# Three edits to the first microseconds of a linear-attention and MLP kernel: a table load put first on ScalarE, one weight load moved to SyncE's queue, and fewer filler products

## The chip, the core and the metric

The kernel runs on one core of one Trainium2 chip. The metric is the device time of one execution in microseconds (us); the time of a kernel is the median of its runs. A profile is one further execution, taken with the hardware profiler, and it has a time of its own. In the profile PE is TensorE (PEld its weight loads), DVE is VectorE, ACT is ScalarE, POOL is GpSimd and SP is SyncE. A name with a q behind it (SPq, ACTq) is the engine's sequencer, which issues DMAs. The granted TensorE clock is 1.000 in the profiled execution.

## What is computed

```python
x = A_x                                     # [1, 2048, 640], bf16
g = _sigmoid((x * gate_w).sum(-1, keepdims=True))
a = _A_ref(x, A_wqkv, A_wo)                 # linear attention, 32 heads of 20
b = _B_ref(x, B_w1, B_w2, B_w3, B_w4)       # layernorm, w1, gelu, shifted columns, w2, layernorm, w3, gelu, w4
return g * a + (1 - g) * b

# in _A_ref:
phi = lambda t: jnp.where(t > 0, t + 1, jnp.exp(t)) + 1e-6
pq, pk = phi(q), phi(k)
kv = jnp.einsum("bhsd,bhse->bhde", pk, v)
...
```

All inputs are bf16. The products with `wqkv`, `w1`, `w2`, `w3` and `w4` fill TensorE's time. The exponential in `phi` is the first function that ScalarE needs, and it needs a table for it; the gelu of the second half needs another.

## The kernel before, in words

**Tiles.** The 2048 rows of `x` are 16 tiles of 128 tokens. `x_tok[:, t, :]` holds tile `t` with tokens on the partitions, and `xT` holds the same data turned, 640 = 5 slices of 128 features by 2048 tokens. `wq` and `wkg` hold the q and k columns of `wqkv`, each in 5 slices of 128 rows. A q tile is 5 products (one for each slice) of 512 columns, summed in one PSUM bank. The remaining 128 columns of `wq` come later as one strided load.

**Who issues the first loads.** The program writes the DMA issues of the first tiles out by hand (lines 714 to 739). `load_x(t)` always issues on SP. `load_wq(k, queue)` and `load_wk(k, queue)` issue on the queue that is named. Each engine's sequencer issues in the order of the program, and each DMA has a semaphore of its own, on which its first reader waits. SP's order is x tile 0, x tile 1, `wq` slice 2, x tile 2, `wkg` slices 0 and 2, x tile 3, `wkg` slice 4, x tile 4. ACT's order is `wq` slices 0, 1, 3 and 4, `wkg` slices 1 and 3, and then the strided rest of `wq`. An x tile and a `wkg` slice are 160 KB each, and a slice of `wq` is 128 KB. From tile 3 on the tiles are turned by DMA transposes (`x_turn`, line 711), also on SP, each of which waits for its tile.

**What TensorE does meanwhile.** `warmup(WARM, ...)` (line 896) multiplies constants into a PSUM bank that nobody reads: with `WARM` = 3456 it is six products of 512 columns and three of 128. `t_x(t)` (line 798) turns tiles 0, 1 and 2 on TensorE (five 128x128 transposes each, against `ident`), and DVE copies the result from PSUM to `xT`. `q_three` (line 949) runs the first three q tiles in an order written out by hand:

```python
order = [(0, 0), (1, None), (0, 1), (1, 0), (1, 1), (0, 2), (1, 2), (0, 3), (1, 3), (2, None), (0, 4), (1, 4),
         (2, 0), (2, 1), (2, 2), (2, 3), (2, 4)]
```

A pair (t, k) is the product of tile `t` with slice `k` of `wq`, and (t, None) is `t_x(t)`. `stream` (line 926) issues them in this order, and TensorE does them in it, so each entry waits for what its own operands need and holds up all behind it. `k_two` (line 958) does the same for the first two k tiles with `wkg`, and `k_tile` and `q_tile` follow, one tile after another.

**The order of the rest.** `_Items.run` (line 336) orders the remaining work by a small cost model (`_Sched.simulate`): the stream A, in which the start lies, keeps its own order, and the other streams are put between by estimated times. `activation` (line 669) tells the model that the first Exp and the first Gelu cost 1290 ns more, for the load of the table. The instruction that loads the table, ACT_TABLE_LOAD, stands in ACT's program directly before the first activation that needs it.

The lines that the change and the prediction touch are 714 to 739, 795, 798, 896 and 949. DMA issues all have line 285 in the profile, since a helper records them (transposes 281); PE's fillers have line 904, its transposes 637, and the products of `stream` 942.

Of the kernel before, what the change touches and what calls it, by code (L numbers as in the profile page):

```python
# [6 lines left out]
F32 = mybir.dt.float32  # L7
ACTF = mybir.ActivationFunctionType
# [408 lines left out]
def _build(nc, A_x, A_wqkv, A_wo, B_w1, B_w2, B_w3, B_w4, gate_w, out, dbg=None, stop=None):  # L417
# [66 lines left out]
    junk = pa.alloc("junk", [128, 1, D], BF16)  # L484
# [78 lines left out]
    def nfree(ap):  # L563
        n = 1
        for d_ in ap.shape[1:]:
            n *= d_
        return n

    def in_psum(ap):
        return ap.tensor.name == ps.name  # L570

    def act(fn, reads, writes, cost=None):
        if cost is None:
            n = nfree(writes[0])
            cost = max(150.0, 100.0 + 0.833 * n + (70.0 if (reads and in_psum(reads[0])) else 0.0))
            cost += 45.0 * max(0, len(reads) - 1)
        return sch.op("act", fn, reads, writes, cost=cost)

    def dve(fn, reads, writes, cost=None):
        if cost is None:  # L580
            n = nfree(writes[0])
            cost = 65.0 + n / 0.96
        return sch.op("dve", fn, reads, writes, cost=cost)
# [85 lines left out]
    def activation(out_ap, in_ap, func, scale=1.0, bias=0.0, accum=None):  # L669
        rd = [in_ap] + [a for a in (scale, bias) if not isinstance(a, (int, float))]  # L670
        wr = [out_ap] + ([accum] if accum is not None else [])
        n = nfree(out_ap)
        cost = max(150.0, 100.0 + 0.833 * n + (70.0 if in_psum(in_ap) else 0.0)) + 45.0 * (len(rd) - 1)
        if accum is not None:
            cost += 91.0
        st_ = ACT_SET.get(func)
        if st_ is not None and st_ != sch.act_func:
            cost += 1290.0
            sch.act_func = st_
        if accum is not None:  # L680
            return act(lambda e: e.activation(out_ap, in_ap, func, bias=bias, scale=scale, accum_out=accum), rd, wr, cost=cost)  # L681
        return act(lambda e: e.activation(out_ap, in_ap, func, bias=bias, scale=scale), rd, wr, cost=cost)  # L682
# [16 lines left out]
    def dma_in(out_ap, in_ap, key, **kw):  # L699
        return sch.dma("sp", out_ap, in_ap, key, **kw)  # L700

    def load_x(t):
        dma_in(x_tok[:, t, :], x2[128 * t:128 * (t + 1), :], "x%d" % t)

    def load_wq(k, queue):
        sch.dma(queue, wq[:, k, 0:512], A_wqkv[128 * k:128 * (k + 1), 0:512], "wq%d" % k)
# [6 lines left out]

    gwr = xn[:, 1, 0:128]
    dve(lambda e: e.memset(gwr, 0.0), [], [gwr])
    load_x(0)
    load_wq(0, "act")
    load_x(1)
    load_wq(1, "act")
    load_wq(2, "sp")  # L720
# [71 lines left out]
        assert tags.get((buf, sl)) == what, ("stale ring slot", buf, sl, what, tags.get((buf, sl)))  # L792

    IT = _Items()
    WARM = 3456
    WARM2 = 128

    def t_x(t):
        for k0, k1 in ((0, 1), (1, KD)) if t < 2 else ((0, KD),):
            b = bank()  # L800
            tr_group(b, [x_tok[:, t, 128 * k:128 * (k + 1)] for k in range(k0, k1)])
            if t == 2:
                mm_group(ps[:, b, 448:448 + KD], [(gwr, ident[:, 0:KD])])
            for j0, j1 in {(1, 1): ((1, 3), (3, KD)), (2, 0): ((0, 1), (1, 3), (3, KD))}.get((t, k0), ((k0, k1),)):
                copy(dve, xT[:, j0:j1, 128 * t:128 * (t + 1)], psb(b, 128 * (j0 - k0), 128 * (j1 - k0)).rearrange("p (k c) -> p k c", k=j1 - j0))
            if t == 2:
                copy(dve, wkg[:, :, D + 1:D + 2], ps[:, b, 448:448 + KD].rearrange("p (k o) -> p k o", o=1))
# [88 lines left out]
    def warmup(cols, cyc):  # L896
        b = bank()
        one = nc.const_aps.tensor(1.0, [128, 512], BF16)
        steps = [512] * (cols // 512) + [128] * (cols % 512 // 128)

        def fn(e):
            ins = None
            for n in steps:
                ins = e.matmul(ps[:, b, 0:n], one[:, 0:128], one[:, 0:n], start=True, stop=True)
            return ins
        pe(fn, [], [ps[:, b, :]], cost=cols * cyc)
# [54 lines left out]
    def addA(name, dur, fn, deps=()):  # L961
        IT.add("A", name, dur, fn, deps)

    addA(("warm",), 0.0, lambda: warmup(WARM, 0.834))
    addA(("tx", 0), 0.28, lambda: t_x(0))
# [485 lines left out]
def bass_gated_mix__linear_attn_block__mixer_s_mlp__prompt_kernel(  # L1451
    nc, A_x, A_wqkv, A_wo, B_x, B_w1, B_w2, B_w3, B_w4, gate_w, out
):
    assert tuple(A_x.shape) == (1, S, D) and tuple(out.shape) == (1, S, D)
    assert tuple(A_wqkv.shape) == (D, 3 * D) and tuple(A_wo.shape) == (D, D)
    assert tuple(B_w1.shape) == (D, D) and tuple(B_w2.shape) == (D, D)
    assert tuple(B_w3.shape) == (D, F) and tuple(B_w4.shape) == (F, D) and tuple(gate_w.shape) == (D,)
    _build(nc, A_x, A_wqkv, A_wo, B_w1, B_w2, B_w3, B_w4, gate_w, out)
# [28 lines left out]
```

## Time and profile before

| what | value |
|---|---|
| runs | 258.79 us median of 3 (258.46 to 259.11) |
| the profiled execution | 259.12 us, of it a span of 257.9 us from the first to the last instruction |
| busy | PE 254.6 us (99% of the span), DVE 144.1, ACT 108.5, POOL 90.6 |
| chain that ended last | PE 96%, DMA 2% |
| first DMA issues | 0.79 us on SP and on ACT |
| fillers | 0.83 us to about 3.7 us |
| ACT_TABLE_LOAD, the first of two | 4.14 us, 1.28 us long |
| first Exp | 8.01 us |

The span is cut into instructions of each engine. Times in the timeline count from the span's start. A DMA issue has a start and a length on the sequencer (0.40 to 0.46 us for these), and apart from it a time to landing, from the start of the issue to the last step of its semaphore. The chain that ended last is followed back from the last instruction; what stands in it sets the end, and other work has slack.

### The profile page before, as it was taken

The page shows a single profiled execution, that of the slowest core. Times are in us where ns is not written, and L with a number is a line of the kernel's source. Part 1 is how long each engine was busy: PE and PEld are TensorE (multiplying, and loading weights), DVE is VectorE, ACT ScalarE, POOL GpSimd, SP SyncE. Part 2 cuts the span into 40 slices and gives each one's busy share as a digit, 9 for nine tenths or more (in the row PEclk, how much of TensorE's full clock was granted, in tenths as well). Part 3 has the DMA queues.
Part 4 walks back from the last instruction along what each step waited for, and adds up shares of the span by engine and source line. Part 5 has one row for each costly group of instructions (what it writes and reads, how often), then busy time and mean ns, then how long its engine had stood idle before and what let it go on. Part 6 is the DMA issues. An engine that isn't in the chain of part 4 may idle for free.

```text
span 257.9 us, 3612 instructions
## 1 busy us (share of the span) xinstructions
PE 254.6 (99%) x1418; PEld 110.6 (43%) x1242; DVE 144.1 (56%) x290; ACT 108.5 (42%) x222; POOL 90.6 (35%) x146
## 2 busy tenths in 40 slices
PE   8999999999999999999999999999999999999997
PEld 4333333344454333334444444444444444444444
DVE  2697888899953995489999400689300043200033
ACT  1486676751356867665854230003520100253000
POOL 5021399967762153758907100423000011300000
DMA  6767698545843699362915520022300112200002
GB/s 209 223 170 197 145 144 223 172 86 127 108 99 78 97 335 382 85 106 51 124 40 127 127 54 20 0 82 73 51 0 0 23 20 102 102 1 3 0 20 102
DMA packets 57825, 26.48 MB, mean 103 GB/s; under 512 B 49188, under 2 KB 56397, under 8 KB 57808
## 3 DMA queue, kind: packets, MB, share of 16 engines
q1 hardware_dynamic: 54976, 21.87, 35.9%
q0 software_dynamic: 1168, 3.28, 4.9%
q10 hardware_dynamic: 1664, 1.11, 1.4%
q8 instruction: 10, 0.16, 0.3%
q14 instruction: 7, 0.06, 0.1%
HBM read 12.04 MB, written 2.62 MB: 57 GB/s over the span
## 4 chain that ended last, share of the span: by engine, by line
PE 96%; DMA 2%; SPq 0%; DVE 0%; issue 0%
PE ps L606 37%; PE ps L1240 30%; PE ps L625 14%; PE ps L831 7%; PE ps L614 4%; DMA x_tok<-in_A_x_dram 2%; PE ps L942 1%; PE ps L1286 1%; PE ps L1147 1%; SPq L285 0%; PE ps L1029 0%; PE ps L1058 0%; PE ps L637 0%; DVE x_tok L665 0%
## 5 line engine op out<-in xcount | busy, mean ns | idle before, releaser
L606 PE MATMUL ps<-xnT,w 128*128 128x512 bf16 x360 | 81.3, 379 | 0.0
L665 DVE SCALAR_TENSOR_TENSOR x_tok<-ps,stg,abx 128x512 bf16<-128x512 f32 (+2 forms) x17 | 12.2, 719 | 81.5 <-PE ps L1240 81.3
L682 ACT ACTIVATE h2T<-ps 128x512 bf16<-128x512 f32 x52 | 30.6, 598 | 59.3 <-PE ps L606 59.3
L606 PEld LDWEIGHTS ps<-xnT,w 128*128 128x128 bf16 x360 | 34.5, 98 | 41.6 <-issue 2.2
L1240 PE MATMUL ps<-w,h2T 128*128 128x512 bf16 (+2 forms) x221 | 45.4, 366 | 0.0
L648 POOL TENSOR_SCALAR xn<-x_tok,st 128x640 bf16<-128x640 bf16 x32 | 35.3, 1110 | 27.8 <-DMA xnT<-xn 27.2
L648 POOL TENSOR_SCALAR abx<-x_tok,stg 128x640 f32<-128x640 bf16 (+1 forms) x16 | 14.8, 930 | 70.0 <-DVE x_tok L665 70.0
L1240 PEld LDWEIGHTS ps<-w,h2T 128*128 128x128 bf16 x221 | 21.1, 98 | 24.1
L682 ACT ACTIVATE Er<-ps 128x512 bf16<-128x512 f32 (+1 forms) x36 | 23.0, 648 | 14.8 <-PE ps L614 10.6
L681 ACT ACTIVATE junk<-x_tok 128x640 bf16<-128x640 bf16 x32 | 23.6, 738 | 3.9 <-DVE x_tok L663 3.7
L682 ACT ACTIVATE hsT<-ps 128x512 bf16<-128x512 f32 (+1 forms) x32 | 19.0, 593 | 12.6 <-PE ps L606 12.1
L625 PE MATMUL ps<-w,hsT 128*128 128x512 bf16 x80 | 23.0, 379 | 0.0
L625 PE MATMUL ps<-wkg,xT 128*128 128x512 bf16 x70 | 20.6, 379 | 0.0
L663 DVE SCALAR_TENSOR_TENSOR x_tok<-ps,x_tok 128x640 bf16<-128x640 f32 x16 | 13.2, 822 | 10.8 <-PE ps L614 10.2
L1240 PE MATMUL ps<-M_sb,pqnT 128*128 128x512 bf16 (+2 forms) x85 | 18.6, 367 | 0.0
L831 PE MATMUL ps<-pk_tok,x_tok 128*128 128x512 bf16 x80 | 17.8, 379 | 0.0
L614 PE MATMUL ps<-wkg,xT 128*128 128x130 bf16 x80 | 17.6, 220 | 0.0
L1176 DVE TENSOR_TENSOR pq_tok<-pq_tok,dnr 128x300 bf16<-128x300 bf16 (+1 forms) x48 | 17.3, 415 | 0.6
L614 PE MATMUL ps<-w,hsT 128*128 128x128 bf16 x80 | 17.5, 219 | 0.0
L606 PE MATMUL ps<-wq,xT 128*128 128x512 bf16 x65 | 16.2, 379 | 0.0
L648 DVE TENSOR_SCALAR Er<-Er 128x512 bf16<-128x512 bf16 (+1 forms) x36 | 12.2, 340 | 6.8 <-ACT Er L682 5.9
L656 DVE TENSOR_TENSOR qprod<-qprod,pk_tok 128x640 f32<-128x640 f32 x13 | 15.1, 1165 | 0.4
(90 smaller groups left out, 252.4 us busy)
## 6 DMA issues: line engine op xcount, KB each, us to landing
w<-in_B_w_dram SPq DMA_DIRECT2D x1, 2160.0 KB, 8.1
w<-in_B_w_dram SPq DMA_DIRECT2D x1, 2080.0 KB, 13.1
out_dram<-x_tok SPq DMA_DIRECT2D x3, 640.0 KB, 3.1
w<-in_B_w_dram POOLq DMA_DIRECT2D x8, 160.0 KB, 3.4
x_tok<-in_A_x_dram SPq DMA_DIRECT2D x6, 160.0 KB, 4.1
x_tok<-in_A_x_dram SPq DMA_DIRECT2D x1, 960.0 KB, 5.5
wv<-in_A_wqkv_dram POOLq DMA_DIRECT2D x1, 800.0 KB, 5.3
x_tok<-in_A_x_dram SPq DMA_DIRECT2D x1, 640.0 KB, 5.0
```

What stands on the lines that cost most here:

```text
L606: ins = e.matmul(out_ap, l, r, start=(i == 0), stop=(i == n - 1))
L614: return e.add_instruction(mybir.InstMatmult(name=nc.get_next_instruction_name(), engine=e.engine, ins=[e.lower_ap(r), ll], outs=[e.lower_ ...
L625: e.matmul(outs[0], l, r, start=st, stop=sp, skip_group_check=True)
L648: return engf(lambda e: e.tensor_scalar(out_ap, in_ap, s1, s2, op0, op1), rd, [out_ap], cost=cost)
L656: return engf(lambda e: e.tensor_tensor(out_ap, a, b_, op), [a, b_], [out_ap], cost=cost)
L663: return dve(lambda e: e.scalar_tensor_tensor(out_ap, in0, scalar, in1, op0, op1, accum_out=accum), rd, [out_ap, accum], cost=cost + 70.0)
L665: return dve(lambda e: e.scalar_tensor_tensor(out_ap, in0, scalar, in1, op0, op1), rd, [out_ap], cost=cost)
L681: return act(lambda e: e.activation(out_ap, in_ap, func, bias=bias, scale=scale, accum_out=accum), rd, wr, cost=cost)
L682: return act(lambda e: e.activation(out_ap, in_ap, func, bias=bias, scale=scale), rd, wr, cost=cost)
L831: ins = e.matmul(o, l, r, start=(t0 + q_ == 0), stop=(t0 + q_ == NT - 1))
L1176: dve(lambda e, o=o, i0=i0, i1=i1: e.tensor_tensor(o, i0, i1, ALU.mult), [i0, dnr[:, 1, sd, :]], [o], cost=cost)
L1240: ins = e.matmul(o, l, r, start=first and i == 0, stop=last and i == len(prs) - 1, skip_group_check=True)
```

## The change

ScalarE's program gets one activation in front: an Exp of one constant column (128x1) into `junk`, which nobody reads. With it the table load moves from behind ACT's seven DMA issues to before them. The load of `wq` slice 0 goes from ACT's queue to SP's, behind x tile 0 and ahead of x tile 1. `WARM` becomes 3200, which is six products of 512 columns and one of 128.

```diff
     gwr = xn[:, 1, 0:128]
     dve(lambda e: e.memset(gwr, 0.0), [], [gwr])
+    activation(junk[:, 0, 0:1], nc.const_aps.tensor(0.0, [128, 1], F32), ACTF.Exp)
     load_x(0)
-    load_wq(0, "act")
+    load_wq(0, "sp")
     load_x(1)
     load_wq(1, "act")
     load_wq(2, "sp")
...
     IT = _Items()
-    WARM = 3456
+    WARM = 3200
     WARM2 = 128
```

SP's order is then x tile 0, `wq` slice 0, x tile 1, `wq` slice 2, x tile 2, `wkg` slices 0 and 2, and so on; ACT's is table load, Exp, `wq` slices 1, 3 and 4, `wkg` slices 1 and 3, the strided rest of `wq`.

## The prediction

> **What bounds the kernel now.** I read the page's chain first, then the chain at the start in order of time.
>
> ```profile
> ## 4 chain that ended last, share of the span: by engine, by line
> PE 96%; DMA 2%; SPq 0%; DVE 0%; issue 0%
> ```
>
> ```profile
> 2.18 5.05 DMA x_tok<-in_A_x_dram
> 7.23 0.05 issue
> 7.28 0.45 PE ps L637 x5
> ```
>
> From 7.28 us on the chain is nearly all PE, and the page has PE busy 99% of the span: whatever moves PE's work at 7.28 moves the end by as much. What PE waits for there is x tile 2, which SP issues at 2.18 and which lands at 7.23. PE itself shows the wait:
>
> ```profile
> 7.28 0.45 PE L637 MATMUL ps<-ident,x_tok 128*128 128x128 bf16 x5 [0.55 <-DMA x_tok<-in_A_x_dram]
> 7.57 0.17 PE L606 MATMUL ps<-ident,xn 128*128 128x5 bf16 x1
> 7.60 1.74 PE L942 MATMUL ps<-wq,xT 128*128 128x512 bf16 x7
> ```
>
> PE was idle for 0.55 us (by modelled ends; the last product before, (1,3), starts at about 6.35, so by starts it could have gone on at 6.57). So everything before 7.28, fillers included, has slack, and the question is when x tile 2, or another operand, lands. Next the two issuing queues, in order of time:
>
> ```profile
> 0.79 0.87 SPq L285 DMA_DIRECT2D x_tok<-in_A_x_dram  x2
> 1.71 0.43 SPq L285 DMA_DIRECT2D wq<-in_A_wqkv_dram  x1
> 2.18 0.43 SPq L285 DMA_DIRECT2D x_tok<-in_A_x_dram  x1
> 2.66 0.91 SPq L285 DMA_DIRECT2D wkg<-in_A_wqkv_dram  x2
> ```
>
> ```profile
> 0.79 1.86 ACTq L285 DMA_DIRECT2D wq<-in_A_wqkv_dram  x4
> 2.69 0.94 ACTq L285 DMA_DIRECT2D wkg<-in_A_wqkv_dram  x2
> 3.65 0.46 ACTq L285 DMA_DIRECT2D wq<-in_A_wqkv_dram  x1
> 4.14 1.28 ACT L682 ACT_TABLE_LOAD   x1 [4.14 <-issue]
> 8.01 1.09 ACT L682 ACTIVATE Er<-ps 128x512 bf16<-128x512 f32 x2 [2.59 <-PE ps L942]
> ```
>
> Each issue takes about 0.46 us, and the table load lies in ACT's idle time: its first Exp waits for PE until 8.01, 2.59 us after the load is over. Last, the DMA view narrowed to one issue at a time (here SP's third, fourth and fifth: the last number is the time to landing), and the stretches of the windows view:
>
> ```profile
> wq<-in_A_wqkv_dram SPq DMA_DIRECT2D x1, 128.0 KB, 3.6
> ...
> x_tok<-in_A_x_dram SPq DMA_DIRECT2D x1, 160.0 KB, 5.1
> ...
> wkg<-in_A_wqkv_dram SPq DMA_DIRECT2D x1, 160.0 KB, 5.5
> ```
>
> ```profile
> 3.20:4.00 0.80, 0.80 (x7) 0.55 (x6) 0.00 (x0) 0.00 (x0) 0.65 (x4) 1.00 1.01 342
> 4.00:4.80 0.80, 0.80 (x9) 0.59 (x8) 0.56 (x2) 0.66 (x1) 0.72 (x5) 1.00 1.00 292
> 4.80:5.60 0.80, 0.80 (x9) 0.42 (x6) 0.79 (x4) 0.62 (x1) 0.00 (x0) 1.00 0.89 253
> ```
>
> The last two columns are the share of the DMA engines and GB/s. With a share of 0.9 to 1.0 the loads are bound by the DMA engines, not by their issue. Issue plus time to landing gives SP's landings: x0 3.7, x1 4.4, wq2 5.3, x2 7.2, wk0 8.1 or 8.2, wk2 8.9, x3 9.5, wk4 10.1 us; and ACT's, read in the same way: wq0 3.8, wq1 4.6, wq3 5.6, wq4 7.5, wk1 8.3, wk3 9.1, the rest of wq 10.9 us. Two queues side by side each land one DMA in about 0.6 to 1.9 us, so a DMA's time is its place in its own queue.
>
> **The change, part by part.**
>
> *wq0 on SP.* SP gets one issue more ahead of x1, wq2 and x2. x2 becomes SP's fifth DMA and takes the place of wk0. The bytes say the same: before, SP's first five are 160+128+160+160+160 = 768 KB, after, 160+128+160+128+160 = 736 KB; ACT's first five are 672 KB before and, one place further on, 384+160+160 = 704 KB after. Both sums are 1440 KB. So x2 lands where wk0 does now, 8.1 instead of 7.23: +0.9 us. A second chain ends at the same moment: wq2 takes x2's place, 7.2, and behind it PE still has (0,2), (1,2), (0,3), (1,3), four products at 0.216 us from start to start, to 8.1. This is why x2 being asked for by issue only 0.47 us later is not the price: the lower bound is 0.47, the upper one the place of wk0 by its rounded row, 2.66+5.5-7.23 = 0.93, and I take 0.9, since the DMA engines' share is near 1. Behind it nothing is late: wk0 then lands at 8.9 and is first read at 9.18+0.9, wk4 at 10.6 (x4's place) and is read at about 11.1+0.9; x3 lands at 10.1, its transpose took 2.5 us to land, and q tile 3 starts at 13.26+0.9.
>
> The Trainium skill, "DMA: Bandwidth & Descriptors", section "Issuing engines are not separate DMA queues", says that transfers from all issuing engines share the same DMA engines, and that the issuing engine decides only over the sequencer's time. By that alone this part would cost one issue, +0.47 us instead of +0.9, and the whole would stay within 0.3%.
>
> *Table load first.* It takes 1.28 us off ACT at 4.14, where ACT was idle, so nothing is won there. It puts 1.28 us and an Exp of one column (nearest row: the 128x2 activation at 12.16, 0.17 us) ahead of ACT's issues. Does ACT's sequencer wait for them? No DMA stands behind an ACT compute instruction in the early trace. The nearest row: a semaphore instruction of ACT's sequencer ends at 13.1 us while the Exp that starts at 12.93 runs to 13.63. The sequencer goes on while the engine works. I therefore take about nothing for the issues: wq1 goes out at 0.8 to 0.9, into wq0's old place. The other end, 1.28 us and more, is the first rival; the table load is another kind of instruction than the Exp, so that end stays likely.
>
> *256 columns of filler fewer.* Two products of 128 columns, which start 0.11 us apart while the clock is still slow: PE is free 0.21 us earlier, at about 3.5. x0 lands at 3.7 as before, so the 0.21 us become a wait for x0; and if x0 came earlier, the gain would end at x2's wait. Cost nothing, cover the wait for x2. The fillers' other effect is the clock: 512 columns start 0.43 us apart up to 3.35, and 0.216 apart from 4.95 on, and weight loads fall from 151 to 98 ns at about 4.3. In the forecast PE also idles from about 4.4 to 5.3 (x1 in wq2's place). If that put the fast clock off, the products before 8.1 would hide it; behind 8.1 each would cost 0.2 us more. I price this at nothing, with up to +0.4 us in the range (two products).
>
> *The planner's costs* move by 1290 ns on ACT and 0.2 us on PE at the start. Stream A keeps its order, and from the middle on all engines are shifted alike; I take nothing, and 0.2 us either way.
>
> Sum: +0.9 us. The profiled execution has 259.12 (span 257.9 and 1.2 around it), so it would have 260.0; it lies 0.33 above the median of the runs. On the median, 258.79+0.9 = 259.7 us. What a measurement of this kernel can tell from no change is about 0.3%, 0.78 us.
>
> **The rivals.**
>
> *First, faster: the table load holds ACT's issues.* Then ACT issues wq1 at 0.79+1.28 = 2.07, and SP has the DMA engines almost alone until about 3.1 us (wq0, issued at 0.79, needed 3.0 us). x0, wq0, x1 land early, and x2 before it is needed. wq1 lands at 2.07+3.0 = 5.1, about when (0,1) ran (4.95); wq3 and wq4 follow after 288 KB each of the two queues' traffic, at some 360 GB/s 0.82 us: 5.9 and 6.7. (0,3) and (1,3) end by 6.5, `t_x(2)` runs without a wait, and (0,4) starts at 6.75 instead of 7.60: -0.85 us, 257.9. PE's own work sets the floor: 6.57 plus the 0.32 us from 7.28 to 7.60, less 0.21 of filler, is 6.7. If wq4 keeps its old gap behind wq3 (1.9 us), (0,4) is at 7.6 or later and the gain is none, so this rival's price runs from -0.95 to 0. For it speaks that the load at 68.30 starts 0.02 us after the Activation before it ended, as if the sequencer waited for the engine (plain Activations of that stretch stand no further apart); against it the semaphore row. It decides from a delay of ACT's issues of about 1 us on.
>
> The Trainium skill, "ScalarE: Activation LUTs", section "What ACT_TABLE_LOAD costs", gives 1.28 us for the load and 1.38 us of drain with it, 2.66 in all; the trace shows 1283 ns and no drain. An estimate by that page would put wq1's issue at 3.45, wq4 at 8.1 and this rival 0.5 us slower than before instead of faster.
>
> *Second, no change: the load disturbed the transfers.* Between 4.0 and 5.6, about where the table load ran (4.14 to 5.42), the rate fell from 342 to 292 and 253 GB/s. DVE's copies ran there as well. If the load was the cause, its move gives back (50+89) GB/s x 0.8 us = 111 KB, at 350 GB/s 0.32 us, and the sum is +0.9-0.3 = +0.6, 259.4 us.
>
> **How the numbers follow.** The forecast has 0.52, and with its bounds (+0.5 to +1.3) 0.42 of that is over 0.78 us and 0.10 within. The first rival has 0.38: 0.28 beyond 0.78 us, 0.10 within. The second has 0.10, 0.05 within, 0.03 slower, 0.02 faster where the relief adds to the first. That makes 0.30 faster, 0.25 within 0.3%, 0.45 slower. The range reaches from the first rival's -0.95 (257.8) to the forecast's +1.3, which is 0.9 and the clock's 0.4 (260.1); the forecast's own range is 259.3 to 260.1.
>
> **What would show it.** Forecast: ACT's first DMA issue starts by 1.0 us, wq2 lands near 7.2, x2 near 8.1, and the first transposes of `t_x(2)` start there instead of at 7.28, the rest shifted alike. First rival: ACT's first issue starts after 2.0 us, x2 lands before 6.5, and PE's wait, if any, is for wq3 or wq4. Second: the first DMA issue is early and the rate between 4.0 and 5.6 stays over 320 GB/s. The prediction is wrong altogether if the chain's first long wait is neither x2 nor a slice of wq, or if PE's time from `t_x(2)` to the end changes by over 0.3 us.

## The result, and the profile after

The changed kernel takes 261.35 us (median of 10 runs, 259.57 to 262.01), the kernel before 258.91 us in the 10 runs beside it. The ratio is 1.0073, with a 95% interval of 1.0051 to 1.0095, which is 1.9 us slower (1.3 to 2.5); by the medians it is 2.4 us, because most runs of the changed kernel are in the upper one of two groups. The forecast was 0.9. The groups are 3 runs at 259.57 to 259.68 us and 7 at 261.05 to 262.01. The runs before have no second group (258.32 to 259.42). The profiled execution, 261.42 us with a span of 260.1, is of the upper group.

The page's chain, and then the chain at the start in order of time (start, length, what):

```profile
PE 94%; DMA 2%; ACT 2%; DVE 1%; issue 1%; SPq 0%
```

```profile
1.71 4.78 DMA x_tok<-in_A_x_dram
6.49 0.05 issue
6.54 0.71 PE ps L637 x5
7.25 2.59 PE ps L943 x7
```

The DMA that ends PE's wait is now the one issued at 1.71, x tile 1. Behind it PE is the chain from 6.54 on: tile 2's transposes, which ended the wait before, come after the products without a wait. PE's own view (start, length, what, and the idle time ahead of it) shows two things:

```profile
4.47 0.58 PE L943 MATMUL ps<-wq,xT 128*128 128x512 bf16 x1 [0.18 <-DMA wq<-in_A_wqkv_dram]
6.54 0.71 PE L637 MATMUL ps<-ident,x_tok 128*128 128x128 bf16 x5 [1.49 <-DMA x_tok<-in_A_x_dram]
7.04 2.79 PE L943 MATMUL ps<-wq,xT 128*128 128x512 bf16 x7
9.68 0.44 PE L637 MATMUL ps<-ident,x_tok 128*128 128x128 bf16 x5
9.95 0.17 PE L606 MATMUL ps<-ident,xn 128*128 128x5 bf16 x1
9.98 1.74 PE L943 MATMUL ps<-wq,xT 128*128 128x512 bf16 x7
```

PE idles 1.49 us for tile 1. Then seven products of 512 columns take 2.79 us behind tile 1 and seven others 1.74 us behind tile 2, and five transposes 0.71 and 0.44 us. Behind tile 1 the products start 0.43 us apart up to 9.18 us, as the fillers of 512 columns do at the start, and behind tile 2 mostly 0.22 us apart. This is what "half speed" and "slow clock" mean here: until about 9.2 us TensorE takes twice the time for the same work. Tile 2's transposes start at 9.68 instead of 7.28, and the first k product at 11.56 instead of 9.18.

ACT's issues did not wait for the table load:

```profile
0.79 1.28 ACT L682 ACT_TABLE_LOAD   x1 [0.79 <-PEq L1473]
0.86 1.35 ACTq L285 DMA_DIRECT2D wq<-in_A_wqkv_dram  x3
```

And in the DMA view, one issue at a time, these are SP's third and fifth, x tiles 1 and 2 (issued at 1.71 and 2.66, so they land at 6.5 and 7.9):

```profile
x_tok<-in_A_x_dram SPq DMA_DIRECT2D x1, 160.0 KB, 4.8
...
x_tok<-in_A_x_dram SPq DMA_DIRECT2D x1, 160.0 KB, 5.2
```

Where all of the time went is seen by holding each profiled execution's time against the start of its first k product (line 942 or 943 with `wkg`, in PE's timeline):

| profiled execution | time, us | first k product | difference |
|---|---|---|---|
| before | 259.12 | 9.18 | 249.94 |
| changed | 261.42 | 11.56 | 249.86 |
| e1, wq0 on SP alone | 261.34 | 11.52 | 249.82 |
| e2, table first alone | 258.14 | 8.32 | 249.82 |
| e3, filler alone | 259.95 | 10.13 | 249.82 |
| e4, changed with filler 3456 | 261.63 | 11.81 | 249.82 |
| e12, the same, another execution | 259.70 | 9.83 | 249.87 |
| e5, changed, TensorE kept busy | 260.50 | 10.68 | 249.82 |
| e6, filler 1280 | 260.42 | 10.59 | 249.83 |
| e7, ACT's issues held | 259.73 | 9.76 | 249.97 |
| e8, gate load late | 261.47 | 11.63 | 249.84 |
| e9, tile 2 third | 259.09 | 9.25 | 249.84 |
| e10, tile 2 fifth | 259.46 | 9.63 | 249.83 |
| e11, the same with fillers | 260.46 | 10.64 | 249.82 |

The difference is the same within 0.15 us. Whatever happens ahead of the first k product reaches the end one to one, and the time behind it did not change, so the planner's altered costs show no price. The small shares of ACT and DVE in the chain after are thus no loss.

### The profile page after: what moved, and what is told of

It reads as the page before. It is cut to its first block, busy times and chain, and to the rows that moved or that the text cites. A ratio compares the mean times of both kernels' runs of the same rounds, so it can differ in the third digit from the quotient of the medians.

```text
span 260.1 us, 3582 instructions
## 1 busy us (share of the span) xinstructions
PE 254.1 (98%) x1389; PEld 110.9 (43%) x1240; DVE 143.9 (55%) x290; ACT 108.7 (42%) x223; POOL 89.8 (35%) x146
## 4 chain that ended last, share of the span: by engine, by line
PE 94%; DMA 2%; ACT 2%; DVE 1%; issue 1%; SPq 0%
PE ps L606 35%; PE ps L1241 30%; PE ps L625 13%; PE ps L832 7%; PE ps L614 4%; PE ps L943 2%; DMA x_tok<-in_A_x_dram 2%; PE ps L1287 1%; ACT hsT L682 1%; PE ps L1148 1%; PE ps L1030 0%; PE ps L1059 0%; PE ps L637 0%; DVE Er L648 0%; ACT junk L681 0%
## 5 line engine op out<-in xcount | busy, mean ns | idle before, releaser
L606 PE MATMUL ps<-xnT,w 128*128 128x512 bf16 x348 | 79.9, 379 | 0.6 <-issue 0.2
L648 POOL TENSOR_SCALAR xn<-x_tok,st 128x640 bf16<-128x640 bf16 x32 | 34.6, 1086 | 27.3 <-DMA xnT<-xn 26.7
L625 PE MATMUL ps<-wkg,xT 128*128 128x512 bf16 x66 | 19.7, 379 | 0.0
```

What stands on the lines that cost most here:

```text
L606: ins = e.matmul(out_ap, l, r, start=(i == 0), stop=(i == n - 1))
L625: e.matmul(outs[0], l, r, start=st, stop=sp, skip_group_check=True)
L648: return engf(lambda e: e.tensor_scalar(out_ap, in_ap, s1, s2, op0, op1), rd, [out_ap], cost=cost)
```

## Experiments

The theory to test, called queue and clock: wq0 ahead of tile 1 makes tiles 1 and 2 land late (the queue's part), and the idle time that this opens on TensorE keeps or puts its clock at half speed for some of the runs (the clock's part). Against it stand the fewer fillers, the early table load, and the late landings alone. e1 to e4 ran side by side (kernel before: 259.02 us), so did e5 to e8 (259.16), and e9 to e11 (258.96).

**e1: wq slice 0 on SP, nothing else.**

```diff
-    load_wq(0, "act")
+    load_wq(0, "sp")
```

> Only wq slice 0 goes to SP; no early table load, filler 3456. Queue-and-clock theory: the queue order is the whole cause, so x tile 1 lands after 5 us and x tile 2 near 8, TensorE idles over 1 us before tile 1, and the time is that of the changed kernel, 259.5 to 262 us (259.6 where the clock stays fast, 261.4 where it does not). Filler theory (the 256 columns decide whether the clock rises): 259.6 us in all runs. Table theory (the early table load costs the time): 258.9 us.

Measured: 260.51 us (259.96 to 261.49), ratio 1.0062 (1.0038 to 1.0086), three runs at 259.96 to 259.98 and three at 261.05 to 261.49. In its profile tile 1 lands at 6.4 us and tile 2 at 8.0, PE idles 1.42 us, and the seven products behind tile 1 take 2.89 us. This one edit brings both groups and most of the loss (0.62% of 0.73% by the ratios, with 3 runs of 6 in the upper group against 7 of 10).

**e2: the table load first, nothing else.**

```diff
+    activation(junk[:, 0, 0:1], nc.const_aps.tensor(0.0, [128, 1], F32), ACTF.Exp)
     load_x(0)
```

> Only the early Exp and with it the table load first; wq slice 0 stays on ACT, filler 3456. Queue-and-clock theory: ACT's first issue at about 0.86 instead of 0.79 us, all landings as before, 258.9 us +-0.4. Table theory: 259.7 us or more.

Measured: 258.89 us (258.14 to 259.60), ratio 0.9998 (0.9984 to 1.0012). Within -0.4 to +0.3 us the early table load costs nothing and brings nothing; a gain as small as the second rival's 0.3 us is not excluded by this run.

**e3: the filler cut, nothing else** (`WARM = 3200`).

> Only the filler is cut to 3200 columns; queues and table as before. Queue-and-clock theory: TensorE waits 0.2 us for x tile 0, the clock rises before 5 us, x tile 2 still ends the wait: 258.9 us +-0.4. Filler theory: the clock rises later in most runs, 260 us or more.

Measured: 259.29 us (258.74 to 259.95), ratio 1.0016 (1.0004 to 1.0028): 0.27 us slower, within the range expected of queue and clock and well under the filler theory's 260. In its profile, from the upper end of its runs, product (0,0) takes 0.63 us and the seven behind tile 1 2.03 (before: 0.48 and 1.78), and wq slices 2 and 4 land at 6.1 and 8.6 us. How much of the 0.27 us is the clock and how much late landings is not settled.

**e4: the changed kernel with its filler back at 3456.**

> The changed kernel with its filler back at 3456 columns. Queue-and-clock theory: x tile 1 still lands after 5 us and TensorE still idles, so 259.5 to 262 us with a median near 261. Filler theory: the clock stays fast, 259.6 us in all runs.

Measured: 260.00 us (259.52 to 261.76), ratio 1.0050 (1.0029 to 1.0071), 8 runs at 259.52 to 260.03 and 4 at 261.56 to 261.76. The filler theory, all at 259.6, falls: the upper group is there with all of the filler. Three of the 4 upper runs list a mean granted clock of 0.993, and all 8 others 1.000; of the changed kernel's 7 upper runs one does (262.01). The median came out 1 us under the expected 261, because the upper group is rarer, 4 of 12 against 7 of 10 with 3200 columns. That the fillers shift the odds fits, but these counts do not prove it.

**e12: one more execution of e4's kernel**, to see the lower group.

> One more execution of the changed kernel with its filler at 3456 columns, whose runs lay in two clusters, 8 at 259.5 to 260.0 us and 4 at 261.6 to 261.8; its first profile was of the upper one. Queue-and-clock theory: if this execution is of the lower cluster, its queues land as in the first profile (x tile 1 near 6.3, tile 2 near 8.0 us), but the products behind tile 1 start 0.22 us apart all along and the first k product starts near 9.9 instead of 11.8 us. Landing theory (the clusters are early and late landings): tile 1 or tile 2 lands over 1 us earlier than in the first profile.

Measured: 259.70 us, of the lower group. PE's timeline of this execution, and then of e4's first profile, which is of the upper group:

```profile
4.29 0.39 PE L943 MATMUL ps<-wq,xT 128*128 128x512 bf16 x1
6.01 0.45 PE L637 MATMUL ps<-ident,x_tok 128*128 128x128 bf16 x5 [1.33 <-DMA x_tok<-in_A_x_dram]
6.30 1.80 PE L943 MATMUL ps<-wq,xT 128*128 128x512 bf16 x7
7.94 0.44 PE L637 MATMUL ps<-ident,x_tok 128*128 128x128 bf16 x5
8.22 0.17 PE L606 MATMUL ps<-ident,xn 128*128 128x5 bf16 x1
8.25 1.74 PE L943 MATMUL ps<-wq,xT 128*128 128x512 bf16 x7
```

```profile
4.55 0.38 PE L943 MATMUL ps<-wq,xT 128*128 128x512 bf16 x1 [0.16 <-DMA wq<-in_A_wqkv_dram]
6.37 0.45 PE L637 MATMUL ps<-ident,x_tok 128*128 128x128 bf16 x5 [1.44 <-DMA x_tok<-in_A_x_dram]
6.66 2.64 PE L943 MATMUL ps<-wq,xT 128*128 128x512 bf16 x7
9.09 0.74 PE L637 MATMUL ps<-ident,x_tok 128*128 128x128 bf16 x5
9.62 0.21 PE L606 MATMUL ps<-ident,xn 128*128 128x5 bf16 x1
9.69 2.28 PE L943 MATMUL ps<-wq,xT 128*128 128x512 bf16 x7
```

In this upper execution the fall is on record in the windows view too (the column third from the end is the granted clock):

```profile
7.20:8.00 0.80, 0.80 (x4) 0.36 (x4) 0.15 (x1) 0.00 (x0) 0.00 (x0) 0.71 1.15 357
8.00:8.80 0.80, 0.80 (x4) 0.29 (x2) 0.00 (x0) 0.00 (x0) 0.00 (x0) 0.50 1.11 365
```

In stretches of 0.4 us it reads 1.00 up to 7.20, 0.50 from 7.60 to 10.80 and 1.00 from 11.20 on, so about 3.4 us were at half the clock, from about 7.5 to 10.9. In e12 it reads 1.00 up to 12 us.

From tile 1's transposes to the first k product it is 9.83-6.01 = 3.82 us in the lower group and 11.81-6.37 = 5.44 in the upper: 1.62 us. The landing of tile 1 makes 0.36 us of the 1.98 between the two. Tile 2 landed 1.0 us earlier too (7.3 against 8.3), which goes against the expectation that all landings stay and lies at the edge of what the landing theory asked for. But PE reaches tile 2 after its landing in both, and at the lower execution's pace (1.93 us from tile 1's transposes to tile 2's) the upper one would have reached it at 8.30, so this landing does not make the difference. In the upper execution the clock was fast for (0,0), 0.38 us, and fell afterwards; in the changed kernel's profile and in e1's, (0,0) is slow already, 0.58 us.

**e5: the changed kernel with TensorE kept busy in the wait for tile 1.**

```diff
-        order = [(0, 0), (1, None), (0, 1), ...
+        order = [(0, 0)] + [(None, None)] * 12 + [(1, None), (0, 1), ...
```

> The changed kernel with 24 more filler products of 128 columns on TensorE between product (0,0) and the transposes of x tile 1, where it idles for 1.5 us; queues unchanged. Queue-and-clock theory: TensorE stays busy, the clock that rose at 4.4 us stays fast, the cluster of runs at 261.5 us vanishes and what is left is the queue's part: all runs between 259.3 and 260.3 us, median 259.8. Queue-alone theory (tile 1 and tile 2 land late and that is all of the loss): no gain, 261 us or more in two runs of three.

Measured: 260.27 us (259.80 to 260.50, 6 runs), ratio 1.0046 (1.0031 to 1.0060). The queues are unchanged, PE does 24 products more, and yet the kernel is faster than the changed one: against the kernel before beside each it is +1.1 us instead of +2.4 by the medians, and +1.2 instead of +1.9 by the ratios. No run lies above 260.50, while all 6 runs of e8 beside it, which keeps the idle time, lie above 260.6. PE's timeline:

```profile
4.63 2.41 PE L905 MATMUL ps<-const-bfloat16-1.0 128*128 128x128 bf16 x24
6.88 0.44 PE L637 MATMUL ps<-ident,x_tok 128*128 128x128 bf16 x5
7.16 1.59 PE L943 MATMUL ps<-wq,xT 128*128 128x512 bf16 x6
```

The fillers start 0.11 us apart up to 6.44 us and 0.06 us apart behind it, and everything behind tile 1 is fast (the trace lacks one of the seven products). They also overstay: tile 1 had landed at 5.9, and its transposes start at 6.88. That is why the median is 0.5 us over what was expected. Late landings alone cannot explain a gain from added work.

**e6: the kernel before with a short filler** (`WARM = 1280`).

> The kernel before with 1280 instead of 3456 columns of filler, so that TensorE idles from about 1.9 us until x tile 0 lands at 3.7; queues unchanged. Queue-and-clock theory: the landings stay, the clock rises only at about 7 us, the products before x tile 2 are at half speed and end after it has landed: 259.3 to 260.5 us. Queue-alone theory: the wait for x tile 2 hides it, 258.9 us.

Measured: 260.50 us (259.27 to 260.64), ratio 1.0049 (1.0030 to 1.0068). The short filler costs 1.3 us with the old queues, and in the profile products start 0.43 us apart from 5.14 to 8.32 us, the wait for wq slice 2 aside. But there wq slice 2 landed at 7.0 us and tile 2 at 8.4, against the expectation that the landings stay. Tile 2's transposes start at 8.71, so of the 1.41 us by which the first k product is later at most 0.3 us is the clock and the rest is late landings. Why they are late with fewer fillers is open, and the run does not show a price of the clock.

**e7: ACT's issues held behind the Exp**, which is the first rival made real.

```diff
-    activation(junk[:, 0, 0:1], nc.const_aps.tensor(0.0, [128, 1], F32), ACTF.Exp)
+    first_exp = activation(junk[:, 0, 0:1], nc.const_aps.tensor(0.0, [128, 1], F32), ACTF.Exp)
...
-    load_wq(1, "act")
+    sch.dma("act", wq[:, 1, 0:512], A_wqkv[128:256, 0:512], "wq1", deps=[first_exp])
```

> The changed kernel with ACT's first DMA made to wait until the early Exp is done, so that ACT's issues start at about 2.35 us as in the prediction's first rival. By that rival's price x tiles 1 and 2 land before 6 us, TensorE waits for wq slices 1, 3 and 4, and the time is 258.0 us (257.8 to 258.9). Queue-and-clock theory: the same landings, but TensorE idles for wq slice 1 until about 5.1 us; under 1 us of idle keeps the clock, 258.0 to 259.0 us; if it does not, 259.5 or more.

Measured: 259.60 us (259.21 to 261.11), ratio 1.0026 (1.0009 to 1.0044): slower than before by 0.44 us, not 0.85 us faster, with 2 of the 12 runs at 261.1. ACT's first issue starts at 2.32 us. The landings are not those of the rival: wq slices 1, 3 and 4 land at 5.9, 7.2 and 8.2 us instead of 5.1, 5.9 and 6.7, and tile 2 at 7.1 instead of before 6. The rival's price was wrong even under its own condition.

**e8: the gate's load issued later by POOL.** It asks whether that small load's packets make tile 1 late.

> The changed kernel with the small load of the gate's weights issued by POOL after its memsets (about 3.5 us) instead of at 1.3 us. If its 256-byte packets at 3.6 to 4.2 us hold one DMA engine up and make x tile 1 land at 6.4 instead of 5.3, tile 1 lands near 5.3 us, TensorE idles under 1 us, and the time is 259.6 us in all runs. If not, as the changed kernel: 259.6 us in one run of three and 261.5 in the others.

Measured: 261.33 us (260.65 to 262.74), ratio 1.0091 (1.0065 to 1.0116). Tile 1 lands at 6.2 us, within the 5.9 to 6.5 of the other runs with these queues, although the gate's load is issued only at 3.34 us and none of its packets run before 5 us. The gate's load is not the cause.

**e10: tile 2 alone in the fifth place**, wkg slice 0 taking its fourth.

```diff
-    load_x(2)
+    load_wk(0, "sp")
     load_wq(4, "act")
-    load_wk(0, "sp")
+    load_x(2)
```

> The kernel before with x tile 2 and wkg slice 0 changed about on SP, so that tile 2 is SP's fifth DMA as in the changed kernel, while x tile 1, the wq slices and the fillers keep their places. Queue-and-clock theory: tile 2 lands near 8.0 us and the end moves by 0.8 us, 259.8 us; TensorE idles for 1.4 us before it, so part of the runs may have the slow clock behind it and lie over 260.5. If the place in the queue costs only its issue, 259.5 us or less.

Measured: 260.01 us (259.46 to 260.44), ratio 1.0040 (1.0026 to 1.0054): +1.05 us by the medians, near the price of the place (0.8 to 0.9) and twice that of an issue (0.47). The one profile is of the fastest run: tile 2 lands at 7.7 us, 0.4 later than before. PE idled little there, since wq slice 2 came late (6.0 us) and the products start 0.43 us apart up to 6.66, so this profile does not show the place alone. No group above appears.

**e11: the same with fillers ahead of tile 2's transposes.**

> The same with 24 filler products of 128 columns before tile 2's transposes, so that TensorE does not idle there. Queue-and-clock theory: the place alone, 259.6 to 260.0 us in all runs, no cluster above.

Measured: 260.39 us (260.01 to 260.86, 5 runs), ratio 1.0052 (1.0038 to 1.0066). No separate group above, but 0.4 us more than expected and no better than e10. In the profile tile 2 lands at 8.7 us, so the landing of this execution hides what the fillers do. Inconclusive for the clock.

**e9: a version that was to beat both**: tile 2 as SP's third DMA, slice 2 on ACT, slice 3 on SP, and products reordered so that the last slices hold back fewer of them.

> A version that is to beat both: the kernel before with x tile 2 as SP's third DMA, wq slice 2 on ACT (third) and slice 3 on SP (fourth), and the first products in the order (0,0), tile 1's transposes, (0,1), (1,0), (1,1), tile 2's transposes, (0,2), (1,2), (2,0), (2,1), (2,2), (0,3), (1,3), (2,3), (0,4), (1,4), (2,4). The last operands to land (about 7.3 us) then hold back six products instead of the transposes and seven. Queue-and-clock theory: the first k product starts near 8.6 instead of 9.2 us, 258.4 us. If the landings of the slices move by as much, or TensorE idles over 1 us and the clock drops, no gain: 259 us or more.

Measured: 259.00 us (258.48 to 259.51), ratio 0.9999 (0.9987 to 1.0011). No gain: the third places of the two queues land at 6.4 and 6.6 us in its profile, so that tile 2 and slice 2 hold up what the reordering had freed. No version here beats the kernel before.

## Why the prediction was wrong

Two steps failed: the landing of tile 1 in its new place, and with it the path, and the price of the clock.

- **What bounds the kernel.** That the end follows PE's first long wait one to one was right (the table above). But the wait moved from tile 2 to tile 1, which is neither `x2` nor a slice of `wq`: the prediction had named that as a sign of being wrong altogether. Its other sign did not come: from tile 2's transposes to the end it is 251.84 us before and 251.74 after.
- **Tile 1 in wq2's place, 5.3 us: failed.** It landed at 6.5, 6.4, 6.3, 5.9, 6.2 and 6.0 us in the changed kernel, e1, e4, e5, e8 and e12, where as SP's second DMA it landed at 4.3 to 4.6 in all seven profiles with the old place. One issue is 0.46 us; the place cost 1.3 us or more. The row that I read was an early one: wq slice 2 as SP's third landed at 5.3 in the kernel before and 5.1 in e2, but at 6.1, 7.0, 6.0 and 6.1 in e3, e6, e10 and e11. So TensorE idled 1.3 to 1.6 us, not the 0.9 I had put down, and tile 1 ended the wait.
- **The clock, priced at nothing with up to 0.4 us: failed.** I wrote that the products before 8.1 us would hide a late clock. In the changed kernel it is 3.14 us from tile 1's transposes to tile 2's (6.54 to 9.68). From 5.3 that would have ended near 8.5, about the 0.4 us over that the range allowed; from 6.54 it ended at 9.68, and tile 2, which landed at 7.9, hid nothing. An estimate divides the 2.38 us by which the first k product of this execution is later: at the pace of e12, 3.82 us behind tile 1's transposes, it would start at 10.36, so 1.18 us is late tile 1 and 1.20 us the clock. Between e4 and e12 the clock cost 1.62 us. The upper group of the changed kernel is 261.50-259.62 = 1.9 us above its lower one, which has no profile that would tell what part of this is landings. With 7 runs of 10 in the upper group, the median went to +2.4.
- **wq0 on SP: +0.9 us.** The size came out near where the clock stayed fast: the lower groups of the changed kernel, e4 and e1 are 0.7, 0.85 and 1.0 us over the kernel before beside them, and tile 2 landed at 7.9 us in the changed kernel (predicted 8.1). That is in part luck. In e12, the one profile of a lower group, tile 2 had landed at 7.3 and waited for PE until 7.94; what was paid there was tile 1's landing at 6.0. e10, which moves only tile 2, gives +1.05 by the medians, with a profile that does not show the place alone. The Trainium skill's rule in "DMA: Bandwidth & Descriptors", section "Issuing engines are not separate DMA queues", that only the issue's time is at stake, would have made it 0.47 us, an estimate with the issue's time from the trace; it is less than any of these.
- **Table load: nothing.** Right. ACT issued at 0.86 us while the load ran from 0.79 to 2.07, and e2 gives 0.9998. The second rival asked for over 320 GB/s between 4.0 and 5.6 us; with the load long over, the windows view of the changed kernel (last column GB/s) is still slow where it was before.

```profile
4.00:4.80 0.80, 0.62 (x4) 0.13 (x2) 0.45 (x2) 0.00 (x0) 0.73 (x5) 1.00 1.11 306
4.80:5.60 0.80, 0.25 (x1) 0.00 (x0) 0.00 (x0) 0.00 (x0) 0.00 (x0) 1.00 0.88 239
```

e4, e5, e8 and e12, also with the load first, have 185 to 276 GB/s there. Of the profiles with the load first and ACT's issues not held only e2's is over 320, with 364 and 324, in the fastest of its 12 executions (258.14).

- **Filler: nothing.** Nearly right for its own part, +0.27 us (e3). It may also raise the share of slow-clock runs (7 of 10, against 4 of 12 in e4), which is open.
- **The first rival** was wrong in its condition (ACT did not wait) and in its price (e7: +0.4 instead of -0.85), since the slices on ACT landed 0.8 to 1.5 us later than the bytes and the rate had said. By its own floor of 6.7 us its bound is -0.9 us, not the -0.95 that it has.

## What to carry to other kernels

Where TensorE starts at half speed and is kept busy by fillers, as here, a late load can be paid twice: once for its lateness, and once more if the clock stays at or falls to half speed with the idle time in front of it. Price the second with the products that follow, not as a small margin. When a change moves an operand back in its queue, ask of every operand that moved whether it is now the one waited for: here it was tile 1, not tile 2. A landing time read from one profile is one draw, here of a spread of 2 us, so take it from several executions before you decide which transfer is last. A group of runs well above the others is worth one more profile: two executions of one kernel showed the clock's part best.

## What had not been expected of the hardware

- An idle time of 1.42 to 1.56 us ahead of tile 1 went with half speed behind it (the changed kernel, e1, e4 and e8), one of 1.33 us did not (e12). In the changed kernel, e1 and e8 the clock had not risen before; in e4 it had, and it fell. Whether the length of the idle time decides or its moment, no run separates. The Trainium skill, "TensorE: Matmul & The Clock Gate", section "Why this matters for your kernels", warns of gaps above about 3 us between bursts of products; the one in e4 is 1.44 us. Its Part 1 says that the clock follows a free-running window, so that the moment varies between runs, which fits, but no run here shows where such a window begins.
- The granted clock in the windows view tells only a part. It shows the fall in e4, but reads 1.00 in the changed kernel from 6.40 to 8.00 us, where 512-column products start 0.43 us apart, and in the kernel before, whose fillers do so up to 3.34 us. The spacing of the products is the safer sign. The length of weight loads, mostly 0.15 us in slow stretches and 0.10 in fast ones, is less sure: the changed kernel has one of 0.10 us at 7.63, among slow products.
- The third place in SP's queue landed between 5.1 and 7.0 us with both queues running. The rate is lowest from about 4 to 5.6 us in most of the profiles; neither the table load nor the gate's load is the cause, and what is stays open.
